# Local attention ahead of two feed-forward parts: attention recut into stacked 64-query blocks

## The chip, the cores and the metric

The kernel runs on one core of one Trainium2 chip. The time is device microseconds of one execution, as the median of three runs. The core's engines, as the profile names them, are PE (TensorE's products), PEld (its weight loads), DVE (VectorE), ACT (ScalarE), POOL (GpSimd) and SP (SyncE, which issues the transfers). Each works through its own queue in order and waits for the others by semaphores.

## What is computed

```python
def _attn_ref(q, k, v):                      # 2 batches, 8 heads, 576 tokens, 64 columns
    scores = 1.0 / np.sqrt(D) * np.matmul(q, k.transpose(0, 1, 3, 2))
    rel = pos[:, None] - pos[None, :]
    mask_plain = (rel >= 0) & (rel < 32)
    mask_dil = (rel >= 0) & (rel < 128) & (rel % 4 == 0)
    # heads 0 to 3 plain, heads 4 to 7 dilated; softmax of the masked scores; times v

def _moe_ref(x, domain_probs, w1, w2):       # 1152 tokens, 512 columns, 4 experts of 1024
    p = domain_probs / (domain_probs.sum(-1, keepdims=True) + 1e-09)
    for e in range(E):
        out += p[:, e:e + 1] * (np.maximum(x @ w1[e], 0.0) @ w2[e])

def _moe2_ref(x, w_in, w_out):               # 512 to 2048 and back
    h = x @ w_in
    return (h - np.tanh(h)) @ w_out
```

A query sees its own and the 31 keys before it, in a dilated head among the tokens of its own residue modulo 4.

## The kernel before

**Feed-forward.** The two parts together are twelve slices of 512 hidden columns (eight of the experts, four of the second part). The 1152 tokens are three groups of 384 (`T`). A slice's group is four `h_step`s (line 444: hidden block f, 12 products of 384 columns; operands are split into a high and a low part, three products for each of four blocks of input columns `kk`) and four `y_step`s (line 482: hidden block f against the second matrix, into three chunks of 128 tokens, 9 products of 512 columns). A hidden block leaves PSUM through ScalarE and VectorE (lines 451 and 452; in the second part a tanh and its difference, lines 458 to 471). `w_split` (lines 420 and 421) makes the high part of 1024 weight columns on ScalarE and the low part on GpSimd. `order` lists the (slice, group) steps: (0,0), (1,0), (0,1), (1,1) and so on, then slice by slice. `beside` says what is emitted behind each step: loads, splits, `x2_step` (line 520: transposes between the two parts), and attention.

**Attention.** It is cut into four units of rows of four tokens: 96 and 48 rows of the first batch, 48 and 96 of the second. A unit has four plain and four dilated heads. A head's queries are blocks of up to 96, each against a window of block + 32 keys. A `Pair` holds two heads, and each head goes through its stages by slots: `scores` (line 202 or 215, one product per block), the maximum on VectorE, `exps` (line 252, one exponential per block on ScalarE, that also sums), `sums` and the reciprocal (lines 262 and 271), `norm` on GpSimd (line 273), `p_transposes` (line 283) and `values` (line 300), and the result `xT` in high and low part (lines 317 and 318). In the first unit the mask joins the sum on TensorE as a product of an identity with the mask (line 198), in the others VectorE adds it on eviction (line 226). The first unit stands before all feed-forward steps; the other three are spread beside the first of them.

PSUM's eight banks are two `h`, three `y` and three `a`. Eleven products of zeros (line 598) come first.

Of the kernel before, what the change touches and what calls it, by code (L numbers as in the profile page):

```python
# [8 lines left out]
F32 = mybir.dt.float32  # L9
# [19 lines left out]
S = 576  # tokens of a batch  # L29
UNITS = [(0, 0, 96), (0, 96, 48), (1, 0, 48), (1, 48, 96)]  # batch, first row, rows of DIL tokens  # L30


def blocks(W, plain):
    """Blocks of a head of a unit, their queries and their keys."""
    M = BQ if plain else W
    return W * DIL // M, M, M + HALO


def _halves():
    """Each unit's plain heads, then its dilated ones, with their columns in the packed q, k, v."""  # L40
    out, at = [], [0, 0, 0]
    for unit in UNITS:
        for plain in (True, False):
# [12 lines left out]
def tile_local_attention_moe_tanhshrink(  # L56
    ctx: ExitStack,
    tc: tile.TileContext,
    q: bass.AP,  # the parts of a half unit side by side, see _pack
# [22 lines left out]
    xp = ctx.enter_context(tc.tile_pool(name="xp", bufs=NG * KD))  # L82
# [4 lines left out]
    ld = ctx.enter_context(tc.tile_pool(name="ld", bufs=2))  # L87
    sp = ctx.enter_context(tc.tile_pool(name="sp", bufs=3))
    st = ctx.enter_context(tc.tile_pool(name="st", bufs=4))
    ps_h = ctx.enter_context(tc.tile_pool(name="ps_h", bufs=2, space=bass.MemoryType.PSUM))  # L90
    ps_y = ctx.enter_context(tc.tile_pool(name="ps_y", bufs=3, space=bass.MemoryType.PSUM))
    ps_a = ctx.enter_context(tc.tile_pool(name="ps_a", bufs=3, space=bass.MemoryType.PSUM))

    PS = {"h": ps_h, "y": ps_y, "a": ps_a}
# [5 lines left out]
    ident = const.tile([128, 128], F32, name="ident")  # L100
    m_reg = const.tile([BQ, 128], F32, name="m_reg")
    m_first = const.tile([BQ, 128], F32, name="m_first")
    ident_b = const.tile([128, 128], BF16, name="ident_b")
# [72 lines left out]
    class Pair:  # L176
# [11 lines left out]
        def scores(self, a):  # L188
# [34 lines left out]
            if h.plain and first:  # L223
                cuts = [(0, 1, m_first), (1, nb, m_reg)]
# [455 lines left out]
```

## Time and profile before

| | us |
|---|---|
| median of three runs | 700.59 |
| lowest and highest | 698.97, 702.90 |
| span of the profiled execution | 697.1 |
| PE busy in it | 690.6 |
| DVE busy | 328.6 |
| ACT busy | 230.4 |
| POOL busy | 148.6 |

The runs' times and the span are of different executions; the median stands 3.5 us over the span, which begins with the first instruction and ends with the last. The busy time of PE counts the whole of an issued product, also where a neighbour overlaps it.

### The profile page before, as it was taken

The page shows a single profiled execution, that of the slowest core. Times are in us where ns is not written, and L with a number is a line of the kernel's source. Part 1 is how long each engine was busy: PE and PEld are TensorE (multiplying, and loading weights), DVE is VectorE, ACT ScalarE, POOL GpSimd, SP SyncE. Part 2 cuts the span into 40 slices and gives each one's busy share as a digit, 9 for nine tenths or more (in the row PEclk, how much of TensorE's full clock was granted, in tenths as well). Part 3 has the DMA queues.
Part 4 walks back from the last instruction along what each step waited for, and adds up shares of the span by engine and source line. Part 5 has one row for each costly group of instructions (what it writes and reads, how often), then busy time and mean ns, then how long its engine had stood idle before and what let it go on. Part 6 is the DMA issues. An engine that isn't in the chain of part 4 may idle for free.

```text
span 697.1 us, 9305 instructions
## 1 busy us (share of the span) xinstructions
PE 690.6 (99%) x3663; PEld 608.6 (87%) x3663; DVE 328.6 (47%) x599; ACT 230.4 (33%) x572; POOL 148.6 (21%) x106
## 2 busy tenths in 40 slices
PE   9999999999999999999999999999999999999997
PEld 5677788889999999999999999999999999999996
DVE  2258456322122222222222222488788699799433
ACT  3347574421412112122122121143454443344221
POOL 1236441200422112113122032022122122122000
PEclk8589999999999999999999999999999999999999
DMA  7024523000121102101101112032222133220111
GB/s 251 25 65 131 158 84 122 1 0 1 61 90 61 31 30 62 31 31 60 31 31 60 31 50 71 2 100 82 60 92 91 61 101 106 67 92 31 41 51 46
DMA packets 26908, 45.19 MB, mean 65 GB/s; under 512 B 2768, under 2 KB 14032, under 8 KB 26864
## 3 DMA queue, kind: packets, MB, share of 16 engines
q1 hardware_dynamic: 26864, 44.59, 20.3%
q8 instruction: 29, 0.48, 0.3%
q14 instruction: 15, 0.12, 0.1%
HBM read 42.22 MB, written 2.36 MB: 64 GB/s over the span
## 4 chain that ended last, share of the span: by engine, by line
PE 97%; DVE 2%; ACT 0%; issue 0%; DVEq 0%
PE bank_y L482 43%; PE bank_h L444 24%; PE bank_a L444 19%; PE bank_a L300 2%; PE bank_a L215 2%; PE bank_a L202 2%; PE bank_y L300 1%; PE bank_h L202 1%; PE bank_a L283 1%; PE bank_y L283 1%; PE bank_a L198 1%; PE bank_y L598 1%; PE bank_a L520 1%; DVE se L262 0%; PE bank_h L198 0%; DVE s L226 0%
## 5 line engine op out<-in xcount | busy, mean ns | idle before, releaser
L482 PE MATMUL bank_y<-whi,h 128*128 128x512 f32 x864 | 277.3, 393 | 0.0
L482 PEld LDWEIGHTS bank_y<-whi,h 128*128 128x128 f32 x864 | 162.2, 188 | 33.9
L482 PE MATMUL bank_y<-wlo,h 128*128 128x512 f32 x432 | 168.8, 391 | 0.0
L444 PE MATMUL bank_h<-x,whi 128*128 128x384 f32 x640 | 164.1, 337 | 0.0
L444 PE MATMUL bank_a<-x,whi 128*128 128x384 f32 x512 | 130.3, 335 | 0.0
L421 POOL TENSOR_TENSOR wlo<-raw,whi 128x1024 fp32r<-128x1024 f32 x32 | 76.4, 2389 | 238.6 <-ACT whi L420 238.6
L444 PEld LDWEIGHTS bank_h<-x,whi 128*128 128x128 f32 x640 | 115.3, 188 | 2.6
L444 PE MATMUL bank_h<-x,wlo 128*128 128x384 f32 x320 | 107.3, 335 | 0.0
L482 PEld LDWEIGHTS bank_y<-wlo,h 128*128 128x128 f32 x432 | 81.1, 188 | 15.7
L444 PEld LDWEIGHTS bank_a<-x,whi 128*128 128x128 f32 x512 | 92.7, 188 | 1.2
L498 DVE SCALAR_TENSOR_TENSOR acc<-bank_y,pn,acc 128x512 f32<-128x512 f32 x63 | 44.1, 749 | 93.4 <-PE bank_y L482 93.4
L444 PE MATMUL bank_a<-x,wlo 128*128 128x384 f32 x256 | 85.7, 335 | 0.0
L421 POOL TENSOR_TENSOR wlo<-t,whi 128x512 fp32r<-128x512 f32 x32 | 43.5, 1360 | 170.0 <-ACT whi L420 170.0
L452 DVE SCALAR_TENSOR_TENSOR h<-bank_h,h 128x384 fp32r<-128x384 f32 x60 | 33.4, 556 | 97.1 <-ACT h L451 97.1
L451 ACT ACTIVATE h<-bank_h 128x384 fp32r<-128x384 f32 x60 | 29.5, 491 | 146.6 <-PE bank_h L444 144.8
L444 PEld LDWEIGHTS bank_h<-x,wlo 128*128 128x128 f32 x320 | 60.1, 188 | 0.0
L451 ACT ACTIVATE h<-bank_a 128x384 fp32r<-128x384 f32 x36 | 17.7, 492 | 111.8 <-PE bank_a L444 111.8
L444 PEld LDWEIGHTS bank_a<-x,wlo 128*128 128x128 f32 x256 | 48.0, 188 | 0.0
L452 DVE SCALAR_TENSOR_TENSOR h<-bank_a,h 128x384 fp32r<-128x384 f32 x36 | 20.1, 557 | 53.6 <-ACT h L451 53.6
L420 ACT ACTIVATE whi<-t 128x512 fp32r<-128x512 f32 x32 | 20.3, 633 | 73.1 <-DVE t L404 73.1
L398 DVE SCALAR_TENSOR_TENSOR t<-raw,t 128x512 int32<-128x512 int32 x32 | 36.7, 1147 | 1.1
L420 ACT ACTIVATE whi<-raw 128x1024 fp32r<-128x1024 f32 x32 | 33.6, 1052 | 1.4 <-DMA raw<-in_moe_w_dram 1.4
(173 smaller groups left out, 572.6 us busy)
## 6 DMA issues: line engine op xcount, KB each, us to landing
raw<-in_moe_w_dram SPq DMA_DIRECT2D x32, 512.0 KB, 3.8
raw<-in_moe_w_in_dram SPq DMA_DIRECT2D x16, 512.0 KB, 3.6
raw<-in_moe_w_out_dram SPq DMA_DIRECT2D x16, 512.0 KB, 3.3
v<-in_v_dram SPq DMA_DIRECT2D x4, 512.0 KB, 4.2
out_dram<-oacc SPq DMA_DIRECT2D x8, 256.0 KB, 2.1
q<-in_q_dram SPq DMA_DIRECT2D x6, 192.0 KB, 2.6
q<-in_q_dram SPq DMA_DIRECT2D x3, 384.0 KB, 3.3
k<-in_k_dram SPq DMA_DIRECT2D x2, 512.0 KB, 5.3
```

The lines of the kernel that those rows point to most:

```text
L202: nc.tensor.matmul(out=sb[:M, j, :K], lhsT=h.q[r0:r0 + D, self.c, j * M:(j + 1) * M], rhs=h.k[r0:r0 + D, self.c, j * h.step:j * h.step + K ...
L215: nc.tensor.matmul(out=sb[:M, j, :K], lhsT=h.q[r0:r0 + D, self.c, j * M:(j + 1) * M], rhs=h.k[r0:r0 + D, self.c, j * h.step:j * h.step + K ...
L283: nc.tensor.transpose(pb[:K, j * M:(j + 1) * M], self.p[a][:M, j, :K], ident[:M, :M])
L300: nc.tensor.matmul(out=self.xb[D * a:D * a + D, j * M:(j + 1) * M], lhsT=h.v[:K, j, f0:f0 + D], rhs=self.pt[a][:K, j * M:(j + 1) * M], sta ...
L398: nc.vector.scalar_tensor_tensor(out=t, in0=low, scalar=29, in1=t, op0=ALU.logical_shift_right, op1=ALU.bitwise_or)
L420: nc.scalar.activation(out=hi, in_=raw, func=ACTF.Copy)
L421: nc.gpsimd.tensor_tensor(out=lo, in0=raw, in1=hi.bitcast(F32), op=ALU.subtract)
L444: nc.tensor.matmul(out=hb, lhsT=a, rhs=x[:, b_, :], start=(n == 0), stop=(n == 3 * KD - 1))
L451: nc.scalar.activation(out=ht[:, 0, :], in_=hb, func=ACTF.Relu)
L452: nc.vector.scalar_tensor_tensor(out=ht[:, 1, :], in0=hb, scalar=0.0, in1=ht[:, 0, :].bitcast(F32), op0=ALU.max, op1=ALU.subtract,)
L482: nc.tensor.matmul(out=state["y"][c], lhsT=a, rhs=b_, start=(f == 0 and n == 0), stop=(f == NF - 1 and n == 2),)
L498: nc.vector.scalar_tensor_tensor(out=acc[ch], in0=y, scalar=p, in1=acc[ch], op0=ALU.mult, op1=ALU.add)
```

## The change

Attention is cut by batch: plain heads as nine blocks of 64 queries, dilated heads as residues of 64, 64 and 16 rows. Blocks are stacked in pairs on the 128 partitions, so that a head is one tile of 128 x 5 x 96 scores (the tenth place of a plain head repeats its last block). `scores` takes two heads at once and alternates between them, one on the upper and one on the lower 64 rows, each into a bank of its own. The mask is added by VectorE for every unit; the maximum is subtracted by GpSimd; one exponential per head follows, and the sum is taken by VectorE. The transposed products leave through ScalarE alone. All of batch 0 stands before the feed-forward steps, with three of four input blocks of the first two hidden blocks put between its stages (`early_h`); batch 1 stands slot by slot beside the steps of (0,0) and (1,0). `y_step` goes chunk by chunk, all four hidden blocks at once. The banks are two each of `s`, `h`, `y` and `a`. Some weight splits of slice 0 go to VectorE, and the splits of slice 1 stand beside the first four steps.

```diff
-BQ = 96
+BQ = 64
+BK = BQ + HALO
+NST = 5
-UNITS = [(0, 0, 96), (0, 96, 48), (1, 0, 48), (1, 48, 96)]
+ROWS = S // DIL
+CUTS = [(0, BQ), (BQ, BQ), (2 * BQ, ROWS - 2 * BQ)]
...
+        def scores(self):
+            which = self.banks["s"]
+            self.sb = [
+                bank(which)[:, :NST * BK].rearrange("p (j c) -> p j c", c=BK) for _ in range(2)
+            ]
+            for part, j, qs, ks in self.h.scores(self.c):
+                M = qs.shape[1]
+                for a in range(2):
+                    nc.tensor.matmul(
+                        out=self.sb[a][part:part + M, j, :],
+                        lhsT=qs[D * a:D * a + D, :], rhs=ks[D * a:D * a + D, :],
+                        start=True, stop=True,
                     )
+        def largest(self, a):
...
+            nc.vector.scalar_tensor_tensor(
+                out=s, in0=self.sb[a], scalar=SCALE, in1=masks[self.h.plain],
+                op0=ALU.mult, op1=ALU.add,
+            )
+            nm = st.tile([128, NST], F32, tag="nm", name="nm")
+            nc.vector.tensor_reduce(out=nm, in_=s, axis=AX.X, op=ALU.max, negate=True)
+            nc.gpsimd.tensor_tensor(
+                out=s, in0=s, in1=nm.unsqueeze(2).to_broadcast([128, NST, BK]), op=ALU.add
+            )
...
+            nc.scalar.activation(out=p, in_=self.s[a], func=ACTF.Exp)
...
+            nc.vector.tensor_reduce(out=sm, in_=p, axis=AX.X, op=ALU.add)
+            nc.vector.tensor_scalar(out=sm, in0=sm, scalar1=1e-9, scalar2=None, op0=ALU.add)
...
+        def stages(self):
+            yield 7, 0, self.scores
+            for a in range(2):
+                for order, lag, emit in (
+                    (0, 1, self.largest), (1, 2, self.norm), (3, 3, self.p_transposes),
+                    (4, 1, self.exps),
+                ):
+                    yield order, a + lag, lambda emit=emit, a=a: emit(a)
+            yield 2, 5, self.values
...
-    def y_step(s, g, f, state):
...
+    def y_step(s, g, c, state):
+        y = bank("y")
+        for f in range(NF):
+            whi, wlo = wb(s, f)
...
+    EARLY = 2
+    def h_bank(s, g, f):
+        if (s, g) == (0, 0):
+            return "y" if f < EARLY else "h"
+        if s < 2 and g == 0:
+            return "h"
+        return "ha"[(s * NG * NF + g * NF + f) // 2 % 2]
...
+    def early_h(kk):
+        state = states[0, 0]
+        for f in range(EARLY):
+            h_products(0, 0, f, state, [kk])
+            state["done", f] = kk + 1
+    for kk in range(KD - 1):
+        slots[0][2 * kk + 6].append((5, lambda kk=kk: early_h(kk)))
...
+    for t, sc, engine in (
+        (3, early[0], nc.vector), (6, early[1], nc.gpsimd), (9, early[2], nc.vector),
+        (11, early[3], nc.gpsimd),
+    ):
+        slots[0][t].append((6, lambda sc=sc, engine=engine: w_split(*sc, engine=engine)))
+    for i, sc in enumerate(early[4:]):
+        put(i, lambda sc=sc: w_load(*sc))
+        put(i + 1, lambda sc=sc: w_split(*sc))
+    for t, emits in enumerate(slots[1]):
+        for _, emit in sorted(emits, key=lambda e: e[0]):
+            put(t, emit)
```

How the instructions stand on GpSimd around the first feed-forward steps (pn is a scaled tile of probabilities, wlo a low part of weights). Before:

```order
L421 TENSOR_TENSOR wlo_438<-raw_150,whi_437 128x1024
L273 TENSOR_TENSOR pn__503<-p_481,rs_501 96x256
L421 TENSOR_TENSOR wlo_512<-raw_152,whi_511 128x1024
L273 TENSOR_TENSOR pn__542<-p_505,rs_540 96x256
L273 TENSOR_TENSOR pn__565<-p_544,rs_563 96x256
L421 TENSOR_TENSOR wlo_577<-raw_154,whi_576 128x1024
```

One split stands between the scaled tiles there. Now, from the last split of slice 0 on (s is a tile of scores, nm its negated maximum):

```order
L459 TENSOR_TENSOR wlo_630<-raw_452,whi_629 128x1024
L228 MEMSET dq_668 128x32
L229 MEMSET dk_669 128x48
L459 TENSOR_TENSOR wlo_685<-raw_644,whi_684 128x1024
L304 TENSOR_TENSOR s_690<-s_690,nm_692 128x480
L459 TENSOR_TENSOR wlo_714<-raw_688,whi_713 128x1024
L304 TENSOR_TENSOR s_719<-s_719,nm_721 128x480
L326 TENSOR_TENSOR pn__729<-p_695,rs_727 128x480
```

Three splits and two subtractions stand ahead of the first scaled tile of batch 1 (729).

On TensorE the first hidden blocks and the attention beside them, before, from the first unit's last transposes on (L283 transposes, L300 values, L215 scores, L444 hidden blocks):

```order
L283 MATMUL bank_y<-ident,pn__423 128x96 x4
L300 MATMUL bank_y<-pt,v 64x96 x4
L215 MATMUL bank_a<-k,q 96x128 x2
L300 MATMUL bank_y<-pt,v 64x96 x4
L215 MATMUL bank_a<-k,q 96x128 x2
L444 MATMUL bank_h<-x,whi 128x384 x2
L444 MATMUL bank_h<-x,wlo 128x384
```

Scores of one head at a time stood between, and transposes of an earlier head behind each. Now, from the last products of the fourth hidden block of step (0,0) on (L483 hidden blocks, L335 transposes, L525 output chunks):

```order
L483 MATMUL bank_h<-x,whi 128x384 x2
L483 MATMUL bank_h<-x,wlo 128x384
L335 MATMUL bank_a<-ident,pn__729 96x128 x4
L525 MATMUL bank_y<-whi,h 128x512
L525 MATMUL bank_y<-wlo,h 128x512
L525 MATMUL bank_y<-whi,h 128x512 x2
```

The transposes of tile 729 stand between the hidden blocks and the first output chunk of step (0,0).

The start on TensorE, now, behind the products of zeros:

```order
L288 MATMUL bank_s<-pk,pq 64x96 x20
L288 MATMUL bank_h<-pk,pq 64x96 x20
L335 MATMUL bank_a<-ident,pn__220 96x128 x4
L335 MATMUL bank_a<-ident,pn__266 96x128 x4
L343 MATMUL bank_a<-ident,pn__220 96x128
L343 MATMUL bank_a<-ident,pn__266 96x128
L288 MATMUL bank_s<-dk,dq 64x96 x16
L288 MATMUL bank_s<-dk,dq 32x96 x8
L357 MATMUL bank_a<-pt,pv 64x64 x16
```

The third pair's scores stand behind the first pair's transposes; before, scores of six heads stood ahead of the first transposes.

## Rows read from the trace of the kernel before

**Rows 1.** the page: its first line and the chain by engine

```profile
span 697.1 us, 9305 instructions
...
PE 97%; DVE 2%; ACT 0%; issue 0%; DVEq 0%
```

**Rows 2.** windows: length, then each engine's busy us, clock, DMA share, GB/s

```profile
8.00:10.70 2.70, 2.70 (x15) 1.71 (x15) 1.01 (x3) 1.65 (x9) 0.00 (x0) 1.00 1.00 380
10.70:20.00 9.30, 9.30 (x31) 5.41 (x32) 1.95 (x8) 4.33 (x24) 2.07 (x2) 0.50 0.59 196
36.40:41.00 4.60, 4.60 (x25) 3.71 (x24) 3.01 (x8) 1.49 (x8) 2.07 (x2) 0.50 0.38 114
41.40:48.50 7.10, 6.44 (x56) 5.06 (x54) 4.62 (x11) 3.47 (x8) 3.36 (x2) 1.00 0.14 39
48.50:159.40 110.90, 109.97 (x726) 91.85 (x726) 57.57 (x146) 57.50 (x210) 35.21 (x31) 1.00 0.27 81
159.40:692.00 532.60, 532.60 (x2721) 485.81 (x2720) 252.12 (x400) 155.32 (x288) 100.96 (x56) 1.00 0.18 56
```

**Rows 3.** the chain in order of time: start us, us, what

```profile
48.59 2.33 PE bank_h L444 x12
...
159.42 8.34 PE bank_h L444 x48
167.77 8.20 PE bank_y L482 x36
...
691.85 1.78 DVE oacc L508 x3
```

**Rows 4.** TensorE in order of time: first product, and blocks of one head

```profile
4.87 0.26 PE L198 MATMUL bank_a<-m_first_b,ident_b 96*96 96x128 bf16 x1
...
43.92 0.67 PE L215 MATMUL bank_a<-k,q 64*96 64x128 f32 x4
44.52 0.55 PE L283 MATMUL bank_y<-ident,pn__423 96*128 96x96 f32 x4
...
118.98 1.11 PE L215 MATMUL bank_a<-k,q 64*96 64x128 f32 x8
120.02 0.55 PE L283 MATMUL bank_a<-ident,pn__1297 96*128 96x96 f32 x4
120.50 0.87 PE L300 MATMUL bank_a<-pt,v 128*64 128x96 f32 x8
121.30 0.44 PE L444 MATMUL bank_h<-x,whi 128*128 128x384 f32 x1
```

**Rows 5.** groups of instructions by form: busy us, mean ns, idle before

```profile
L421 POOL TENSOR_TENSOR wlo<-raw,whi 128x1024 fp32r<-128x1024 f32 x32 | 76.4, 2389 | 238.6 <-ACT whi L420 238.6
L420 ACT ACTIVATE whi<-raw 128x1024 fp32r<-128x1024 f32 x32 | 33.6, 1052 | 1.4 <-DMA raw<-in_moe_w_dram 1.4
L226 DVE SCALAR_TENSOR_TENSOR s<-bank_a,m_reg 96x512 f32<-96x512 f32 x8 | 5.5, 687 | 5.9 <-PE bank_a L215 5.8
```

**Rows 6.** in order of time: VectorE's small step alone and beside GpSimd

```profile
37.18 0.15 DVE L262 TENSOR_SCALAR se<-sm 96x4 f32<-96x4 f32 x1
37.79 1.04 POOL L273 TENSOR_TENSOR pn__367<-p,rs 96x512 f32<-96x512 f32 x1 [5.02 <-DVE rs L271]
37.98 0.87 DVE L262 TENSOR_SCALAR se<-sm 96x4 f32<-96x4 f32 x1
```

**Rows 7.** in order of time: second part, a group's last hidden block

```profile
585.53 0.39 PE L482 MATMUL bank_y<-whi,h 128*128 128x512 f32 x1
...
586.90 0.53 ACT L470 ACTIVATE h<-gt 128x384 fp32r<-128x384 f32 x1 [0.21 <-DVE gt L462]
...
587.46 0.56 DVE L471 TENSOR_TENSOR h<-gt,h 128x384 fp32r<-128x384 f32 x1
```

**Rows 8.** groups by form: a hidden block's eviction

```profile
L451 ACT ACTIVATE h<-bank_h 128x384 fp32r<-128x384 f32 x60 | 29.5, 491 | 146.6 <-PE bank_h L444 144.8 <-PE bank_a L283 1.9
L452 DVE SCALAR_TENSOR_TENSOR h<-bank_h,h 128x384 fp32r<-128x384 f32 x60 | 33.4, 556 | 97.1 <-ACT h L451 97.1
```

More of the change, by code (lines that the diff above doesn't have):

```diff
@@ L41, in _halves @@
     out, at = [], [0, 0, 0]
-    for unit in UNITS:
-        for plain in (True, False):
+    for b in range(2):
+        for unit, plain in [((b, 0, ROWS), True)] + [((b, *cut), False) for cut in CUTS]:
             out.append((unit, plain, tuple(at)))
@@ L317, in values @@
[L317 to L318 removed]
+            pb = bank(self.banks["t"])
+            for i in range(2):
+                nc.tensor.transpose(pb[:BK, i * 128:(i + 1) * 128], self.p[i][:, n, :], ident)
+            last = sp.tile([128, 256], F32, tag="pl", name="last", bufs=2)
+            nc.scalar.activation(out=last[:BK], in_=pb[:BK, :256], func=ACTF.Copy)
+            self.last = last
@@ new lines, in values @@
+        def values(self):
+            h = self.h
+            xb = [bank(self.banks["x"]) for _ in range(2)]
+            for blk, t, i, o, n in h.values():
+                for a in range(2):
+                    f0 = (2 * self.c + a) * D
+                    pt = self.pt[a][:BK, t:t + n] if t < 512 else (
+                        self.last[:BK, t - 512 + a * 128:t - 512 + a * 128 + n]
+                    )
+                    nc.tensor.matmul(
+                        out=xb[i][D * a:D * a + D, o:o + n],
+                        lhsT=h.v[:, blk, f0:f0 + D], rhs=pt, start=True, stop=True,
+                    )
+            x = xT[self.kk]
+            for i in range(2):
+                (hi, n, r), (lo, _, _) = (h.spans(x[:, j])[i] for j in range(2))
+                src = xb[i][:, :n]
+                if r is not None:
+                    src = src.rearrange("c (r p) -> c r p", r=r)
+                nc.scalar.activation(out=hi, in_=src, func=ACTF.Copy)
+                nc.vector.tensor_tensor(out=lo, in0=src, in1=hi.bitcast(F32), op=ALU.subtract)
@@ new lines, in tile_local_attention_moe_tanhshrink @@
+    kinds = [kind(b) for b in range(2) for kind in (Plain, Dilated)]
+    slots = [[[] for _ in range(SLOTS)] for _ in range(2)]
+    for b in range(2):
+        for n in range(4):
+            banks = {"s": "sh"[n % 2], "t": "a", "x": "a"} if b == 0 else {"s": "s", "t": "a", "x": "a"}
+            for order_, slot, emit in Pair(kinds[2 * b + n // 2], n % 2, banks).stages():
+                slots[b][2 * n + slot].append((order_, emit))
+    def early_h(kk):
[3 more added lines that the diff above has]
+            state["done", f] = kk + 1
@@ L592, in tile_local_attention_moe_tanhshrink @@
         nc.vector.memset(zero, 0.0)
-        for half in halves[:2]:
-            half.load_qk()
-            half.load_v()
+        kinds[0].load_qk(0)
+        kinds[0].load_qk(1)
+        w_load(*early[0])
+        kinds[0].load_v()
+        w_load(*early[1])
         idle = bank("y")
```

495 lines of the change are left out of this document (220 added, 275 removed).

## Prediction

> **What bounds the kernel now.** I read the page's first lines and its chain first, then the stretches, then the chain in order of time. The chain lies on TensorE for 97% of a span of 697.1 us [rows 1], so the question is how long TensorE works or waits in each stage, and nothing else. The stages [rows 2, 3]: until 48.6 us no feed-forward product runs, TensorE does the first unit's attention (a third of all: 96 of 288 rows); from 48.6 to 159.4 the other two thirds stand between feed-forward steps; from 159.4 to 691.9 feed-forward work alone; then 5.2 us of last sums and stores.
>
> The reader should see three more things in these rows. A slice's group costs 8.34 + 8.20 = 16.54 us and they follow without a gap [rows 3]; 36 of them make 595.4. The stretch of 532.4 us [rows 2] holds 32 (529.3), so the transposes between the two feed-forward parts cost 3.1. Four groups (66.2) lie between 48.6 and 159.4, so attention takes 44.7 us there. And the granted clock is 1.00 up to 10.7 us and 0.50 (1.2 GHz of 2.4) from then on, while TensorE's rows leave no idle time; it is back after the stretch from 36.4 to 41, 4.6 us of transposes and value products without masks between them [rows 2]. So the span is 48.6 + 595.4 + 3.1 + 44.7 + 5.2 = 697.0. The median of the runs lies 3.5 us above the profiled span; I add that at the end.
>
> **What an attention product costs at full clock.** Every product with float32 operands is two passes. Four score passes of 128 columns take 0.60 up to the next block, eight take 1.04 [rows 4]: 0.11 a pass, 0.0825 for 96 columns, and 0.16 for the change of block. Four transposes of 96 columns take 0.48 with such a change, 0.08 each, so 0.11 for 128; eight value passes of 96 columns 0.80, so 0.055 for 64. By these passes the products of the two thirds come to 31.4; the other 13.3 of the 44.7 are the edges of 72 blocks (24 heads, three blocks each), 0.19 an edge.
>
> **Batch 1's attention, beside steps (0,0) and (1,0).** The change removes the mask products, widens 128-column windows to pairs of 96 (88 score products a batch: 2 x 20 plain, 2 x 24 dilated) and does two heads a block. Score passes: 88 x 2 x 0.0825 = 14.5. Transposes 40 x 0.11 = 4.4. Value passes: 136 of 64 columns at 0.055 and 32 of 16 at no more than 0.05, 9.1. Sixteen edges 3.0. That is 31.0. Nothing in the rows shows two heads' passes alternating between row halves. The upper end is the row's own 0.0825 a pass; the lower end is 0.055, the shortest pass seen, of the same 64 weight columns. I take 0.0825, the nearer shape.
>
> New waits come on top. GpSimd now subtracts the maximum as well as scaling, and it is in order. Its rows as the change orders them begin with the last split of slice 0, the split of (1,0), the first head's subtraction, the split of (1,1), the second subtraction, then the first scaling. Splits cost 2.39, ScalarE's copy ahead of each 1.05 [rows 5], a GpSimd step of 480 columns 1.0 (1.04 for 512 [rows 6]), an exponential of 480 columns 0.6 (a little over half of that copy of 1024). Counted from the first feed-forward product that completes the early ones, the second hidden block's eviction lets the copy for (1,0) start near 4.0; split to 7.5, subtraction to 8.5, exponential, an eviction (0.5) and the next copy to 10.9, split to 13.3, subtraction and scaling to 15.3. TensorE reaches the first transposes of batch 1 after 0.5 + 3.3 + 0.5 + 2.1 + 3.3 + 2.1 (the rests of two hidden blocks, scores, two whole blocks of 12 x 0.174) and edges, 12.4: a wait of 2.9. The next head's scaling stands behind one more split, near 21.0, while TensorE has only one output chunk (2.7) to do: a wait of 2.4. Three times transposes follow values at once and need the same two banks back, an eviction by ScalarE and VectorE, 1.1 each: 3.3. Batch 1 thus takes 31.0 + 5.3 + 3.3 = 39.6, for half the attention, against 44.7 for two thirds. Whatever TensorE has behind these waits, the output products of step (0,0) among them, is queued, as it is in order.
>
> **The start, with all of batch 0.** Now the stages of eight heads come before the first full feed-forward step, and they are a chain through four engines. VectorE per head: scale and mask 0.65 (0.687 for 512 columns [rows 5]), the maximum the same, later the sum the same and two small steps 0.4; I call these 1.35 and 1.05. The first score product needs half as much again of queries and keys; it starts at 4.87 now [rows 4], I take 5.5. Pair 1's scores end at 8.8, pair 2's at 12.1. VectorE works through heads 1 to 3 until 15.5, then holds for a weight split whose ScalarE copy stands behind a transposed copy and an exponential: 18.7. Heads 4 and 5, after pair 3's scores (to 21.4), their sums and the first values' evictions: 25.3. Heads 3 and 4's transposes wait for those evictions; with them, six early feed-forward products (1.0) and pair 4's scores TensorE is at 31.2. From there VectorE 1.35 + 1.05 + 1.0 + 1.35, head 8's subtraction, exponential, sum and scaling 3.9, pair 3's values to be evicted 1.3, transposes 0.9, ScalarE's two copies round a weight copy 2.65, values 2.6, evictions 2.0: 18.1, so 49.3. A VectorE step of 4 columns took 0.87 beside a GpSimd step and 0.15 else [rows 6]; the change puts such steps beside GpSimd for every head, I add 0.7: 50.
>
> TensorE stands idle from 12.1 to about 17.5 in this chain but for 0.4 of transposes. The clock fell at 10.7 after a stretch that had no gap at all [rows 2], so I let it fall here, and come back, as in the rows, after some 4.6 us of unbroken products: pair 3's scores and pair 1's values (5.9 at full clock) then cost 4 more. The start ends at 54. The 18 feed-forward products that it already does (18 at 8.34 / 48 = 0.174, 3.1) are taken off the later work, and cancel the 3.1 of transposes. Lower end 46 (shorter passes, no fall of the clock). Upper end: all of it at half clock, when TensorE itself binds: 2 x (14.5 + 4.4 + 9.1 + 3.1) + 5.5 + 2 = 69.
>
> **The feed-forward steps in their new order.** An output chunk now takes all four hidden blocks at once. The last block's two halves are ready 1.90 and 2.49 us after the first output product starts [rows 7]; before, products of three chunks covered them, now nine products of 8.20 / 36 = 0.228 (2.05). Weight loads that can no longer run ahead cost about 0.25, in the 12 groups of the second part: 3. At the three groups with transposes the fourth hidden block needs a bank that is still being evicted (0.49 + 0.56 [rows 8]): 1.0 each, 3. Other groups keep their banks in time. Together 6, ends 0 and 12.
>
> **Sum.** 54 + 595.4 + 39.6 + 6 + 5.2 = 700.2, with the 3.5 about 704 us, half a per cent over the median. A measurement of this kernel can tell about that half per cent from no change. Less TensorE work (masks gone, fewer edges) is given back in longer waits at the start.
>
> **Rivals.** First, the two heads' score passes run side by side, so that a pass costs as little as 0.055. For it: they lie on different row halves and banks. Against it: no row has the pattern. The start loses 3, batch 1's scores 4.8, but the wait on GpSimd grows by 2.6, since that chain hardly moves: 699. The Trainium skill, TensorEngine Tiling (Array Packing), under Key Properties and Performance Considerations, states that tiles on different rows can load weights and multiply in parallel, up to twice as fast with 64 rows; no run here shows it yet. By that rule score work would halve rather than lose a third, and most of the rest would go into the same wait on GpSimd, an estimate of 698.
>
> Second, the same and a clock that stays at 1.00, because the early products and denser score blocks fill the gap at 12 to 17 us: the start ends 4 sooner, 695, faster. It decides if the granted clock from 12 to 25 us reads 1.00. For it speaks that the clock held through all later stretches; against it that it fell without any gap.
>
> Third, slower: the clock stays at 0.50 throughout the start and TensorE binds it, up to 69, the sum 719. It decides if pairs take 13 us each or more. Against it: dense stretches brought the clock back at 41 us.
>
> Fourth, the change does not bring its feed-forward products early, as the early blocks wait for a weight split: nothing beyond 3 us either way, inside the forecast's spread.
>
> **Chances.** The forecast 0.47, its own range 697 to 713 (0.20 within half a per cent, 0.27 over); side by side 0.15 (0.11 within, 0.04 faster); side by side at full clock 0.23 (faster); half clock 0.15 (slower). So faster 0.27, same 0.31, slower 0.42. The range from 689 to 718 takes in the second rival with some spread and reaches to the third.
>
> **What would show it.** Right: the first product of step (0,0) that completes a block starts near 54, with a half-clock stretch inside; TensorE waits for GpSimd at batch 1's first two transposes; small waits for hidden blocks in the second part; 16.5 a group in between. Wrong: score passes of two heads overlapping in time, a clock of 1.00 through the start, or an interleaved stretch without waits on GpSimd.

## The result and the profile after

The changed kernel takes **690.0 us** (median of four runs, 689.2 to 690.7) against 700.8 us before (four runs, 699.0 to 702.9): a ratio of 0.984, 95% interval 0.981 to 0.986. It is faster by 1.6%, where 704 was forecast and 0.42 lay on slower. The range from 689 to 718 holds the time at its lower edge.

The page's first line and its chain by engine, as in [rows 1]:

```profile
span 687.9 us, 9361 instructions
...
PE 85%; DVE 6%; DMA 3%; issue 2%; ACT 1%; POOL 1%; SPq 1%; DVEq 0%; POOLq 0%; ACTq 0%
```

TensorE still carries the chain, but 15% of it now lies on others; it was 3%. TensorE in order of time, as in [rows 4] (the bracket is the idle time ahead of a row and what ended it):

```profile
4.76 1.06 PE L288 MATMUL bank_s<-pk,pq 64*64 64x96 f32 x40
...
18.72 1.51 PE L288 MATMUL bank_s<-dk,dq 64*64 64x96 f32 x32 [1.24 <-DMA dk<-in_k_dram]
...
42.72 0.44 PE L483 MATMUL bank_y<-x,whi 128*128 128x384 f32 x1 [0.78 <-ACT x L367]
...
44.98 0.62 PE L483 MATMUL bank_y<-x,whi 128*128 128x384 f32 x2
...
52.85 1.87 PE L288 MATMUL bank_s<-pk,pq 64*64 64x96 f32 x38 [4.67 <-DVE s L298]
...
59.98 0.64 PE L335 MATMUL bank_a<-ident,pn__729 128*96 128x128 f32 x4 [1.31 <-POOL dq L228]
...
65.37 0.64 PE L335 MATMUL bank_a<-ident,pn__801 128*96 128x128 f32 x4 [1.99 <-POOL pn__801 L326]
...
76.50 1.22 PE L288 MATMUL bank_s<-dk,dq 64*64 64x96 f32 x48
...
79.94 1.15 PE L357 MATMUL bank_a<-pt,pv 96*64 96x64 f32 x32
80.92 0.29 PE L357 MATMUL bank_a<-last,pv 96*64 96x64 f32 x4
84.21 0.61 PE L335 MATMUL bank_a<-ident,pn__968 128*96 128x128 f32 x4 [3.00 <-DVE x L368]
...
94.67 0.61 PE L335 MATMUL bank_a<-ident,pn__1097 128*96 128x128 f32 x4 [1.91 <-DVE x L368]
```

Three things are to be seen. The 40 score passes of a plain pair, two passes for each of ten blocks of two heads, take 1.06 us: 0.026 a pass, where the forecast had 0.0825 and a lower end of 0.055. The first product of step (0,0) that completes a hidden block starts at 42.72, not at 54 (the row at 44.98 completes the second hidden block; it serves below as the mark at which the start is over). And the waits of batch 1 are there, at more places than forecast.

The granted clock by stretches, as in [rows 2], and the chain in order of time, as in [rows 3]:

```profile
10.60:27.50 16.90, 11.08 (x110) 8.66 (x110) 11.29 (x22) 7.11 (x14) 8.03 (x11) 0.50 1.00 259
27.70:51.40 23.70, 16.14 (x273) 12.99 (x272) 15.19 (x28) 12.11 (x22) 13.48 (x12) 1.00 0.68 148
51.60:58.20 6.60, 5.35 (x49) 5.13 (x50) 2.70 (x6) 1.10 (x2) 2.53 (x2) 0.50 1.04 302
85.70:88.90 3.20, 3.20 (x14) 3.03 (x13) 0.46 (x1) 0.87 (x3) 0.00 (x0) 0.50 0.00 0
96.00:99.20 3.20, 3.20 (x13) 3.04 (x13) 0.12 (x1) 0.49 (x1) 0.00 (x0) 0.50 0.02 5
```

```profile
7.30 11.29 DMA dk<-in_k_dram
...
109.53 4.18 PE bank_h L483 x24
...
117.88 8.20 PE bank_y L525 x36
...
591.36 8.61 PE bank_y L525 x36
...
675.65 8.39 PE bank_y L525 x36
```

The clock falls near 10.5 us, as it did before, but comes back at 27.6 instead of 41, and falls three more times in batch 1, behind the waits of 4.67, 3.00 and 1.91 above. In the start a transfer stands on the chain for 11 us. From 109.5 us on it is feed-forward work alone, at 16.54 us a group as before, and in the second part an output step takes 8.36 to 8.63 us instead of 8.20.

### The profile page after: what moved, and what is told of

The parts are those of the page before. It is cut to its first block, busy times and chain, and to the rows that moved or that the text cites. A ratio compares the mean times of both kernels' runs of the same rounds, so it can differ in the third digit from the quotient of the medians.

```text
span 687.9 us, 9361 instructions
## 1 busy us (share of the span) xinstructions
PE 652.1 (95%) x3839; PEld 580.4 (84%) x3839; DVE 323.4 (47%) x533; ACT 205.1 (30%) x376; POOL 149.6 (22%) x117
## 4 chain that ended last, share of the span: by engine, by line
PE 85%; DVE 6%; DMA 3%; issue 2%; ACT 1%; POOL 1%; SPq 1%; DVEq 0%; POOLq 0%; ACTq 0%
PE bank_y L525 40%; PE bank_h L483 21%; PE bank_a L483 21%; DMA dk<-in_k_dram 2%; DMA raw<-in_moe_w_dram 1%; PE bank_a L335 1%; DVE t L433 1%; SPq L235 1%; POOL s L304 1%; PE bank_s L288 1%; DVE t L436 1%; DVE acc L537 1%; DVE t L429 1%; PE bank_y L670 1%; ACT h L494 1%
## 5 line engine op out<-in xcount | busy, mean ns | idle before, releaser
L525 PE MATMUL bank_y<-whi,h 128*128 128x512 f32 x864 | 277.5, 394 | 0.0
L525 PEld LDWEIGHTS bank_y<-whi,h 128*128 128x128 f32 x864 | 160.6, 188 | 39.1 <-DVE h L507 3.1
L525 PE MATMUL bank_y<-wlo,h 128*128 128x512 f32 x432 | 169.0, 391 | 0.0
L483 PE MATMUL bank_h<-x,whi 128*128 128x384 f32 x592 | 154.2, 341 | 0.0
L483 PE MATMUL bank_a<-x,whi 128*128 128x384 f32 x544 | 138.7, 335 | 2.6 <-DVE h L495 1.7
L459 POOL TENSOR_TENSOR wlo<-raw,whi 128x1024 fp32r<-128x1024 f32 x30 | 71.7, 2393 | 279.2 <-ACT whi L458 279.2
L483 PEld LDWEIGHTS bank_h<-x,whi 128*128 128x128 f32 x592 | 109.8, 192 | 3.0 <-issue 0.2
L483 PE MATMUL bank_h<-x,wlo 128*128 128x384 f32 x296 | 101.0, 341 | 0.0
L483 PEld LDWEIGHTS bank_a<-x,whi 128*128 128x128 f32 x544 | 98.0, 188 | 3.3 <-DVE h L495 2.2
L525 PEld LDWEIGHTS bank_y<-wlo,h 128*128 128x128 f32 x432 | 81.1, 188 | 15.4
L483 PE MATMUL bank_a<-x,wlo 128*128 128x384 f32 x272 | 90.9, 334 | 0.0
L494 ACT ACTIVATE h<-bank_h 128x384 fp32r<-128x384 f32 x50 | 24.5, 490 | 206.5 <-PE bank_h L483 206.5
L495 DVE SCALAR_TENSOR_TENSOR h<-bank_h,h 128x384 fp32r<-128x384 f32 x50 | 27.8, 557 | 106.6 <-ACT h L494 106.6
L495 DVE SCALAR_TENSOR_TENSOR h<-bank_a,h 128x384 fp32r<-128x384 f32 x44 | 24.5, 558 | 69.0 <-ACT h L494 69.0
L483 PEld LDWEIGHTS bank_h<-x,wlo 128*128 128x128 f32 x296 | 56.8, 192 | 0.0
L483 PEld LDWEIGHTS bank_a<-x,wlo 128*128 128x128 f32 x272 | 51.1, 188 | 0.0
## 6 DMA issues: line engine op xcount, KB each, us to landing
pv<-in_v_dram SPq DMA_DIRECT2D x2, 864.0 KB, 11.3
```

The lines of the kernel that those rows point to most:

```text
L459: (engine or nc.gpsimd).tensor_tensor(out=lo, in0=raw, in1=hi.bitcast(F32), op=ALU.subtract)
L483: nc.tensor.matmul(out=state["bank", f], lhsT=a, rhs=x[:, b_, :], start=(kk == 0 and n == 0), stop=(kk == KD - 1 and n == 2),)
L494: nc.scalar.activation(out=ht[:, 0, :], in_=hb, func=ACTF.Relu)
L495: nc.vector.scalar_tensor_tensor(out=ht[:, 1, :], in0=hb, scalar=0.0, in1=ht[:, 0, :].bitcast(F32), op0=ALU.max, op1=ALU.subtract,)
L525: nc.tensor.matmul(out=y, lhsT=a, rhs=b_, start=(f == 0 and n == 0), stop=(f == NF - 1 and n == 2),)
```

## The experiments

All start from the changed kernel. Times are medians of four or more runs, and differences of 1 to 2 us can lie within their spread (the runs of one kernel lie 1 to 6 us apart); each ratio is to the kernel before, run on the same chip.

| run | us | ratio, 95% interval | mean granted clock, profiled run |
|---|---|---|---|
| changed kernel | 690.0 | 0.984 (0.981, 0.986) | 0.977 |
| heads apart | 696.8 | 0.992 (0.990, 0.995) | 0.969 |
| parts apart | 697.3 | 0.995 (0.993, 0.997) | 0.973 |
| both apart | 714.9 | 1.017 (1.012, 1.022) | 0.953 |
| scores and values apart | 715.7 | 1.020 (1.017, 1.024) | 0.964 |
| weights first | 689.6 | 0.985 (0.981, 0.988) | 0.972 |
| splits behind | 687.0 | 0.982 (0.978, 0.986) | 0.980 |
| tail of groups | 685.8 | 0.979 (0.975, 0.982) | 0.975 |
| filled start | 688.4 | 0.984 (0.980, 0.987) | 0.988 |
| three together | 682.4 | 0.974 (0.969, 0.978) | 0.987 |
| dilated first | 684.3 | 0.976 (0.972, 0.980) | 0.980 |
| filled batch 1 | 677.4 | 0.966 (0.962, 0.971) | 1.000 |
| both apart, filled | 692.1 | 0.987 (0.981, 0.992) | 0.995 |

### Why a score pass is so short: heads apart, parts apart, both apart

```diff
-            for part, j, qs, ks in self.h.scores(self.c):
-                for a in range(2):
+            for a in range(2):
+                for part, j, qs, ks in self.h.scores(self.c):
```

That is heads apart. Parts apart keeps the alternating heads and sorts the blocks, and both apart has the two edits:

```diff
-            for part, j, qs, ks in self.h.scores(self.c):
+            for part, j, qs, ks in sorted(self.h.scores(self.c), key=lambda e: e[0]):
```

> All score products of a pair's first head stand before those of the second, so neighbours differ only in the half of the output partitions they write, no longer in the half of the rows they read. In the changed kernel the 40 passes of a plain pair take 1.06 us, 0.026 each, where the forecast had 0.0825 and a lower end of 0.055. Theory: four quarters of the array work at the same time, two by rows and two by columns; then 40 passes take about 2.1 us here, batch 1's 176 passes 4.4 us more than now, part of it hidden in waits, and the time is 692 to 698. Rival A, a narrow pass is short by itself whatever stands beside it: 1.06 us and 690. Rival B, only rows count: 2.1 us here as well, but 1.06 in the run that keeps the heads alternating.

> Heads alternate as before, but all blocks that write the lower output partitions stand before those that write the upper ones, so neighbours differ in rows alone. Theory of four quarters: 40 passes of a plain pair take about 2.1 us, time 692 to 698. Rival A (a narrow pass is short by itself): 1.06 us, 690. Rival B (only rows count): 1.06 us, 690, while the run with the heads apart is slower. A fourth possibility, only columns count: 2.1 or more here and 1.06 with the heads apart.

> Heads apart and partitions apart: neighbours share rows and columns of the array. Theory of four quarters: one pass at a time, 3.3 us for the 40 passes by the forecast's 0.0825, up to 4.2 if a pass alone is four times 0.026; batch 1's 176 passes then cost 10 to 14 us more than now, the start up to as much, about half of it hidden in waits: 698 to 708. Rival A (a narrow pass is short by itself): 1.06 us and 690. If a time near the forecast's 704 comes out, the forecast failed by the price of a score pass and by little else.

The last dilated pair's 48 passes at a granted clock of 1.00, in the runs with heads apart, parts apart and both apart; the same block of the changed kernel is the 1.22 at 76.50 above:

```profile
80.92 2.28 PE L288 MATMUL bank_s<-dk,dq 64*64 64x96 f32 x48
```

```profile
82.76 2.28 PE L288 MATMUL bank_s<-dk,dq 64*64 64x96 f32 x48
```

```profile
95.88 4.42 PE L288 MATMUL bank_s<-dk,dq 64*64 64x96 f32 x48
```

1.22, 2.28, 2.28, 4.42: take away the alternation of heads or that of output halves, and the block takes 1.9 times as long; take away both, 3.6 times. So passes on four quarters of the array overlap. Rival A (short by itself) and rival B (rows only) are out. The 40 passes of a plain pair, for which 2.1 us were expected with one alternation and 3.3 to 4.2 with none, take 1.60 and 2.69 at full clock, against 1.06. One thing stays open: two heads lie on different row halves and in different banks, and no run puts both row halves into one bank. The Trainium skill, TensorEngine Tiling (Array Packing), under Available Configurations, lists four tiles of 64 x 64, and under Theoretical Speedup gives up to twice for a dimension of at most 64. The rows agree: 1.9 times by one dimension and 3.6 by two, 1.7 and 2.5 for plain pairs. The prediction had taken from that page the rows alone.

Both apart was expected at 698 to 708 and took 714.9. What was not counted is the clock. Windows of that run, two of its seven stretches at 0.50 and the sum of all (the longest, 20.3 us, lies in the start):

```profile
49.30:59.40 10.10, 10.10 (x56) 9.44 (x57) 4.64 (x7) 1.92 (x3) 4.11 (x4) 0.50 0.21 59
...
76.60:90.10 13.50, 13.50 (x63) 9.60 (x61) 2.82 (x6) 1.95 (x4) 6.21 (x5) 0.50 0.15 47
...
sum 63.50, PE 59.38 PEld 50.17 DVE 22.47 ACT 15.28 POOL 24.40; mean PE 8.48 PEld 7.17 DVE 3.21 ACT 2.18 POOL 3.49
```

The seven make 63.5 us at half clock; the four of the changed kernel make 29.9. So it was open how much of the 25 us is passes and how much clock; the last run bounds that.

### Value products

```diff
-            for blk, t, i, o, n in h.values():
-                for a in range(2):
+            for a in range(2):
+                for blk, t, i, o, n in h.values():
```

> As the run with both apart, and the value products of a pair's first head stand before the second's, so that neighbours no longer alternate between the two halves of the output partitions. In the changed kernel 36 value passes of a plain pair take 1.27 us, 0.035 each, where the forecast had 0.055. Theory: column halves overlap in these too, so 36 passes take 2.0 to 2.6 us, batch 1's values 4 to 6 us more than now, and the time is 3 to 8 us over the run with only the scores apart: 702 to 714. Rival A: 1.27 us, and the same time as that run.

The second plain pair of batch 1 in that run (18 + 13 of its 36 passes; the rest stands between them):

```profile
108.24 1.20 PE L357 MATMUL bank_a<-pt,pv 96*64 96x64 f32 x18
...
109.33 0.92 PE L357 MATMUL bank_a<-pt,pv 96*64 96x64 f32 x13
110.09 0.28 PE L357 MATMUL bank_a<-last,pv 96*64 96x64 f32 x2
```

The pair takes about 2.1 us (108.24 to 110.4) instead of 1.27 (79.94 to 81.21 above): 0.058 a pass instead of 0.035. The forecast's 0.055 was the price of a pass that alternates with nothing. The whole kernel lost only 0.8 us by it, less than the spread of the runs (714.5 to 717.3 against 710.0 to 715.9) and below the 3 to 8 expected: the profiled run spends less time at half clock than its neighbour (mean 0.964 against 0.953), and waits for VectorE's evictions ahead of transposes shrink, from 7.0 to 5.2 us in all. What of that is cause and what chance, these runs don't tell.

### The waits of batch 1: weights first, splits behind

```diff
     for i, sc in enumerate(early[4:]):
-        put(i, lambda sc=sc: w_load(*sc))
-        put(i + 1, lambda sc=sc: w_split(*sc))
+        put(i - 1, lambda sc=sc: w_load(*sc))
     for t, emits in enumerate(slots[1]):
         for _, emit in sorted(emits, key=lambda e: e[0]):
             put(t, emit)
+    for i, sc in enumerate(early[4:]):
+        put(i + 1, lambda sc=sc: w_split(*sc))
```

Weights first is the line of the load alone; splits behind is all of it.

> The loads of slice 1's second chunk and of those after it stand one step earlier on SyncE, ahead of batch 1's dilated queries and keys; nothing else moves. In the changed kernel that load is issued at 50.0 us, behind six loads that wait for the buffers of the pair scored at 44 us, lands at 56.6, and the split that needs it ends on GpSimd at 58.0, ahead of the first scaled tile of batch 1. Theory: the load is the releaser there; the split ends before 54, TensorE's wait of 1.31 us ahead of the first transposes goes and the next waits shrink: 2 to 4 us less, 686 to 688. Rival: GpSimd's order alone holds TensorE, its split, two subtractions and a scaling add up anyway, and the scores of the second pair still start near 52.8: 689 to 691.

> As the run with the weights first, and each split of slice 1 stands behind the subtraction, exponential and scaling of its step instead of ahead of them. Theory: in-order GpSimd is the second releaser: the wait of 4.67 us ahead of the second pair's scores, which goes back through an eviction and an exponential to the subtraction behind a split of 2.35, falls by 2 or more, the waits of 1.31 and 1.99 at the first two transposes go, and with shorter gaps the granted clock does not fall at 51.5 us, which costs some 2.6 us now: 683 to 686. Rival: the waits move to VectorE's chain (two maxima, two sums, evictions) and little is left to gain: 687 to 690.

Weights first, GpSimd and then TensorE in order of time:

```profile
53.30 2.35 POOL L459 TENSOR_TENSOR wlo<-raw,whi 128x1024 fp32r<-128x1024 f32 x1 [2.04 <-ACT whi L458]
```

```profile
53.48 1.87 PE L288 MATMUL bank_s<-pk,pq 64*64 64x96 f32 x38 [4.67 <-DVE s L298]
...
65.16 0.64 PE L335 MATMUL bank_a<-ident,pn__801 128*96 128x128 f32 x4 [2.69 <-POOL pn__801 L326]
```

The load is no longer late: the split ends at 55.7 instead of 58.0, though its start of batch 1 is 0.6 us later. The wait of 1.31 is gone, and the next one is 2.69 instead of 1.99: the time is the same. The rival held; the load stood on the chain, but only in parallel with GpSimd's order. The clock has a part in it: behind the 2.69 it fell here (about 65.5 to 69 us), which it did not behind the 1.99. Splits behind:

```profile
51.42 1.87 PE L288 MATMUL bank_s<-pk,pq 64*64 64x96 f32 x38 [4.35 <-DVE s L298]
...
62.28 0.64 PE L335 MATMUL bank_a<-ident,pn__797 128*96 128x128 f32 x4 [1.71 <-POOL pn__797 L326]
```

687.0, at the lower end of the rival's range, and of these 3.0 us the profiled run has 1.1 already at the end of the start (43.9 instead of 45.0), which the edit does not touch; from there to step (0,1) it takes 62.5 us instead of 64.55. The wait of 4.67 fell only to 4.35: the second head's maximum stands on VectorE behind the eviction of a hidden block, which stands on ScalarE behind the first head's exponential. GpSimd's part of the split went behind the subtraction, and the exponential starts 4.4 us after the second hidden block (48.28 - 43.89) instead of 5.7 (50.66 - 44.98), but ScalarE's copy for the same split went between the exponential and the eviction and takes most of that back. ScalarE in that run:

```profile
48.28 0.60 ACT L313 ACTIVATE p<-s 128x480 f32<-128x480 f32 x1 [3.08 <-POOL s L304]
48.80 1.04 ACT L458 ACTIVATE whi<-raw 128x1024 fp32r<-128x1024 f32 x1
49.74 0.47 ACT L494 ACTIVATE h<-bank_h 128x384 fp32r<-128x384 f32 x1
```

No run puts that copy behind the eviction. The clock fell here too, at 50.4 us.

### The second part's output steps

```diff
+        last = NF - 1
...
+        elif c == 0:
+            todo = [(i, f) for i in range(2) for f in range(last)] + [(0, last)]
+        elif c == 1:
+            todo = [(1, last)]
...
+        for i, f in todo:
+            if f == 0:
+                state["y", i] = bank("s" if i == 2 and slices[s][2] is None else "y")
...
-        tb = bank("a")[:, :T]
+        tb = bank("s")[:, :T]
```

> Only in the second part: the first two output chunks of a group take hidden blocks 0 to 2 before either takes the last one, the third chunk and the transposes between the parts write the two banks that scores no longer need. From 109.4 us to the last product 574.7 us pass now, 34 groups of 16.54 make 562.4 and the transposes 3.1: 9.2 us are waits (the forecast had 6). Theory: the 0.16 to 0.43 that a group's output part takes over 8.20 goes (about 3.5 in all), and the three waits of 0.84 to 0.92 behind the transposes (2.6) with it: 5 to 6 us less, 684 to 686. Rival: VectorE's weight decoding holds the evictions there, whatever the banks: 688 to 690.

One group's output step there, chain in order of time:

```profile
604.72 5.62 PE bank_y L535 x24
610.34 2.72 PE bank_s L535 x12
```

8.34 where the same step took 8.6. From the first product of step (0,1) to the last one 569.5 us pass instead of 574.5, and 685.8 us is in the theory's range: the new waits of that stretch cost at least these 5 us (4.2 in the medians).

### The clock of the start: filled start

```diff
+    def fill(n):
+        for _ in range(n):
+            nc.tensor.matmul(
+                out=idle[0].rearrange("p (a b) -> p a b", b=32), lhsT=zero,
+                rhs=zero[:, :32].unsqueeze(1).to_broadcast([128, 16, 32]), start=True, stop=True,
+            )
+    for t, order_, n in ((0, 7.5, 6), (2, 7.5, 10), (3, 3.5, 8), (4, 3.5, 5), (5, 2.5, 5)):
+        slots[0][t].append((order_, lambda n=n: fill(n)))
```

> Products of zeros with all 128 weight columns take the place of those with 32 at the start, and 34 more stand in the gaps of batch 0's first two pairs (at 6, 8.5, 11.7, 15 and 22 us). The granted clock is 0.50 from 10.5 to 27.6 us in the changed kernel. Theory: it falls because TensorE does too little there; with the gaps filled it stays at 1.00 or comes back sooner, the transposes and early products of 23.5 to 27.8 us take half, and the start ends 2 to 4 us earlier: 686 to 688. Rival A: it falls near 10.5 us in any case, as it did before the change without a gap: 690. Rival B: the clock stays up and the chain of loads, VectorE and GpSimd binds all the same: 689 to 690 at a clock of 1.00.

The first eleven products of zeros also go from 32 to 128 weight columns here, so the run does not part that from the filled gaps. The start's window in that run, and where its second hidden block is completed (44.98 in the changed kernel):

```profile
0.00:40.90 40.90, 32.07 (x450) 20.58 (x450) 28.39 (x61) 19.65 (x34) 21.69 (x37) 1.00 0.87 236
```

```profile
41.93 0.62 PE L483 MATMUL bank_y<-x,whi 128*128 128x384 f32 x2
```

The clock stays at 1.00 and the start ends 3.05 us earlier, so it need not fall near 10.5 us: rival A is out. The size is less sure than that. With the start untouched, the same product stands at 43.89 (splits behind), 45.04 (tail of groups) and 45.62 (weights first); with the start filled, at 42.39 (filled batch 1) and 45.48 (three together, below). So where the filling worked it gave some 2.7 us (44.9 on the mean against 42.2), and in one execution of three it did not work. At the end 1.6 us are left (688.4, just over the expected 686 to 688), and the runs overlap (688.0 to 690.5 against 689.2 to 690.7): batch 1 has four stretches at half clock there instead of three.

### Together: three together, dilated first, filled batch 1

> The splits behind, the tail of groups and the filled start together. Alone, their spans were 3.3, 4.3 and 2.0 us shorter than the changed kernel's 687.9, at three different places of the program. If these costs lie one behind the other on TensorE, they add: a span near 678.3, a median of 680 to 682. Rival: the start that ends earlier meets the same loads and splits of slice 1, so that the start's gain is lost in batch 1 again, as in the filled start alone (3.1 us earlier at the end of the start, 2.0 at the end): 682 to 684.

682.4: the rival's range. The three gains don't add fully; 7.1 us of span remain of 9.6. The rival's way is not what the profiled execution shows, though. The start's gain is missing at the end of the start already: the second hidden block is completed at 45.48, the third pair's scores had waited for their transfer until 19.30 (17.15 in the filled start), and the clock fell in spite of the zeros:

```profile
32.30:35.70 3.40, 3.40 (x16) 2.90 (x18) 2.09 (x7) 1.79 (x4) 1.98 (x2) 0.50 0.98 238
```

```profile
45.48 0.62 PE L483 MATMUL bank_y<-x,whi 128*128 128x384 f32 x2
```

From there to step (0,1) pass 62.0 us, as with the splits behind alone (62.5), so batch 1 took nothing of it back.

Dilated first:

```diff
         put_load(b, 0, lambda d=dilated: d.load_qk(0))
+            put_load(0, 0, plain.load_v)
+            put_load(0, 0, lambda: w_load(0, 0))
...
+            put_load(0, 2, lambda: w_load(0, 1))
+            put_load(0, 2, dilated.load_v)
...
-        w_load(*early[0])
-        kinds[0].load_v()
-        w_load(*early[1])
```

> As the three together, and in the start the loads of the first dilated queries and keys stand ahead of the values and of the first two weight chunks (the first split moves back by one step). In the changed kernel these loads are asked for from 5.9 us on, with 1.9 MB ahead of them on the queues, and end at 18.6; the first dilated scores wait for them twice. Theory: the transfers' rate binds that stretch (DMA engines busy above 0.95 of 4.8 to 23.5 us), the order is what can be changed: the first dilated scores are done near 12 to 14 instead of 20.2, VectorE's chain moves up, the start ends 3 to 5 us earlier than with the three together, and so does the end. Rival: VectorE binds (some 20 us of steps for eight heads), the early weights come late in their place: within 1.5 us of the three together.

TensorE and then VectorE in that run:

```profile
15.72 1.22 PE L288 MATMUL bank_s<-dk,dq 64*64 64x96 f32 x48
```

```profile
18.43 1.23 DVE L459 TENSOR_TENSOR wlo<-raw,whi 128x1024 fp32r<-128x1024 f32 x1 [3.15 <-ACT whi L458]
19.58 0.65 DVE L298 SCALAR_TENSOR_TENSOR s<-bank_s,mask_False 128x480 f32<-128x480 f32 x1
```

No gain: 684.3 (681.7 to 685.9), near the rival. The dilated scores are done at 16.9, but the first weight chunk now lands late, its split stands on VectorE ahead of their maximum, and VectorE waits 3.15 us for it. The transfers only changed places. The clock was at 0.50 from about 24 to 27.5 and 31 to 37.5 us in this start, so a part of the loss may be the clock's.

Filled batch 1:

```diff
+    for t, order_, n in ((2, 6.5, 18), (7, 2.9, 12), (9, 2.9, 8)):
+        slots[1][t].append((order_, lambda n=n: fill(n, "y")))
```

That is added to the three together; these products write a bank of `y` that is free there.

> As the three together, and products of zeros also stand in three waits of batch 1 (18 ahead of the second pair's scores, 12 and 8 ahead of the transposes that follow values). In the run with the splits behind, the granted clock fell to 0.50 for 6.8, 3.4 and 3.4 us behind just these waits (50.4, 81.1 and 91.4 us). Theory: it falls because of the waits; with products in them it stays at 1.00, and half of these 13.6 us, less what was waited in them anyway, comes back: 3 to 6 us less than with the three together. Rival A: it falls because of the narrow attention products themselves, fill or not: no gain, or a loss of 1 to 2 by products in the way. Rival B: the clock stays up, but the chain behind the waits (GpSimd, VectorE) binds again: less than 2.

Its windows of the start and of batch 1, and the place of the former wait of 4.67:

```profile
0.00:41.00 41.00, 32.20 (x449) 20.55 (x450) 28.05 (x60) 19.65 (x34) 21.32 (x36) 1.00 0.89 245
41.00:102.00 61.00, 57.42 (x588) 45.67 (x589) 34.18 (x63) 24.07 (x44) 27.73 (x25) 1.00 0.29 92
```

```profile
49.93 1.05 PE L288 MATMUL bank_s<-pk,pq 64*64 64x96 f32 x38 [0.46 <-DVE s L298]
```

677.4, 5.0 below the three together: the theory held. From the end of the start to step (0,1) pass 56.9 us (42.39 to 99.25) instead of 62.0. The clock is 1.00 in the profiled run and 0.993 to 0.997 on the mean of the other three, with the same attention products: at these places it fell because of the waits. That narrow products alone never lower it is not shown; the next run has such a place. This is the fastest version, 3.4% below the kernel before (0.962 to 0.971).

### Passes and clock parted: both apart, filled

> The version with the filled start, the filled batch 1, the splits behind and the tail of groups (677.4 us, clock 1.00 throughout), with the score products of both heads and both output halves apart again. In the changed kernel that edit alone cost 25 us, with 64 us at half clock instead of 30. It parts what the passes themselves cost from what the clock costs. Passes at full clock: 80 plain ones of a batch at 0.061 instead of 0.026 and 96 dilated ones at 0.092 instead of 0.025, 9 us in batch 1 and 9 in the start, of which a third or so takes the place of zero products and waits. Theory: with the waits filled the clock stays near 1.00, and the time is 12 to 18 us over 677.4: 689 to 695. Rival A: the narrow products alone on the array lower the clock whatever stands between: 698 to 704 and a granted clock that falls as often as in the run with both apart. Rival B: the passes are hidden in the waits and the 25 us were the clock's: under 686.

692.1, 14.7 over the same kernel with the heads and parts alternating: the theory's range. One stretch at 0.50 is left (47.9 to 54.5 us). It begins inside a block of score passes in a row, ahead of which TensorE had waited 0.80 and 0.28 us and no more, so there rival A has a point:

```profile
46.38 3.74 PE L288 MATMUL bank_s<-pk,pq 64*64 64x96 f32 x40
```

Groups of score products by form in the run with batch 1 filled (alternating) and in this one (busy us, then mean ns of one):

```profile
L288 PE MATMUL bank_s<-pk,pq 64*64 64x96 f32 x120 | 3.5, 248 | 0.5 <-DVE s L298 0.5
L288 PE MATMUL bank_s<-dk,dq 64*64 64x96 f32 x96 | 2.9, 250 | 0.7 <-DMA dk<-in_k_dram 0.4 <-DVE s L298 0.3
```

```profile
L288 PE MATMUL bank_s<-dk,dq 64*64 64x96 f32 x96 | 10.4, 249 | 0.0
L288 PE MATMUL bank_s<-pk,pq 64*64 64x96 f32 x120 | 9.6, 272 | 0.0
```

One dilated pass lasts the same 250 ns in both (some of the plain ones ran at half clock, hence 272); what differs is how many are under way at once, so the same 96 occupy 2.9 or 10.4 us. Of the 25 us that both apart cost in the changed kernel, about 15 are thus passes in a row, at most 3.3 of them the half clock of the stretch that is left (6.6 us), and about 10 remain, by subtraction, for the clock and the waits behind it.

## Why the prediction was wrong, step by step

**What bounds the kernel.** Right in kind: TensorE, stage by stage. The stages, forecast and measured:

| | forecast | measured |
|---|---|---|
| start, until step (0,0) completes its first block | 54 | 42.7 |
| batch 1 beside steps (0,0) and (1,0), net of their products | 39.6 | 36.8 |
| transposes and new waits from 109.5 us on | 3.1 + 6 | 12.1 |
| last sums and stores | 5.2 | 3.8 |
| median over the span | 3.5 | 2.1 |

Batch 1 is 109.53 - 42.72 less two steps of 16.54 without their early 3.1; 12.1 is 574.5 less 34 groups of 16.54. The differences, -11.3, -2.8, +3.0, -1.4 and -1.4, make the 14 us that the forecast lay over.

**The step that failed: "I take 0.0825, the nearer shape", and its lower end of 0.055.** Passes in a row do cost that: by the blocks of both apart, filled (2.69 us for 40 plain passes and 4.42 for 48 dilated ones), 0.081 on a batch's average. But the change does not issue them in a row. Each neighbour lies on another quarter, and the 176 passes of a batch cost 0.026 each at full clock. In the forecast's own sum this one size takes 10 us off batch 1, and in the start up to 7.6 off pairs 1, 3 and 4 on its chain (3.3 + 3.9 + 3.9 against 1.06 + 1.22 + 1.22): 686, or 689 if the wait on GpSimd grows by the 2.6 of the first rival, instead of 704. The lower end had a place only for passes that shorten each other by a third. Values were mis-sized in the same way: 9.1 us a batch forecast, 5.6 measured (two blocks of 1.27 and two of 1.51).

**The first rival** had the mechanism, but half of it: rows, not columns. Its wait on GpSimd was to grow from 5.3 to 7.9 at the first two transposes. The waits up to there make 7.97 (4.67 + 1.31 + 1.99), but only 3.30 of them end with GpSimd; the 4.67 ends with VectorE, which waits by way of ScalarE for the first subtraction on GpSimd. **The second rival** gave the side and nearly the time (695) for a reason that did not occur: the clock did read 0.50 from 10.6 to 27.5. The run with the start filled shows what it would have been worth, some 2.7 us at the start's end where the forecast took 4.

**Waits and clock in batch 1** were too small, and hid part of the gain. Forecast: products 31.0, waits 8.6, half clock none. Measured: waits of 4.67, 1.31, 1.99, 0.99, 3.00 and 1.91, 13.9; half clock, half of TensorE's 5.35, 3.20 and 3.20 us in the three windows, 5.9; with 0.3 at the first block, 16.7 are left for the products, 14.3 less than forecast: 10 of scores, 3.5 of values, and little of the 3.0 of edges. The two waits that were forecast at the first transposes (2.9 and 2.4) are there, 1.31 and 1.99 long. The largest one, ahead of the second pair's scores, was not foreseen: the pair needs both score banks, and one is held by a maximum behind an eviction, an exponential and a subtraction, which stands behind a split on GpSimd. The forecast has that row of steps (to 10.9 after its mark), but lets it hold only the transposes.

**The start** was forecast as a chain of VectorE, GpSimd and ScalarE. That the third pair's scores would wait for a transfer until 18.6 us was left out: the DMA engines' share stands at 1.00 there, and in the run with the dilated loads first another order only moved the wait to the weights. (The upper end of the start adds up to 69.7, not 69; nothing hangs on it.)

**The new feed-forward order** was right in its two terms, which measure 5.9 against 6: three waits of 0.84 to 0.91 behind the transposes against three of 1.0, and 0.16 to 0.43 a group in the second part against 0.25. The other 3 us lie in the stretch of the transposes (423.92 to 498.82), which the forecast had at 3.1 + 3; no run says what they are. The run on the tail of groups took 5 us out again. The early products came early, so the fourth rival is out; half clock through the whole start, the third, did not come.

## What to carry to other kernels

Products that use a quarter of TensorE's array are priced by what stands beside them: alternate rows and output halves from one product to the next. Here, with a bank of its own for each row half, four passes cost 0.10 to 0.11 us together, where one in a row cost 0.067 (plain) to 0.092 (dilated). When such a change makes TensorE's work shorter, look at once for what it then waits for, since each gap can also cost the clock of what comes behind it; here products of zeros in three gaps gave back more (5 us) than moving the splits that made one of them (2 to 3 us). A price read from a row holds only for the neighbours that the row had.

## What the runs showed of the hardware that was not expected

- Products of at most 64 x 64 on different quarters overlapped with float32 operands: 48 dilated passes of 96 columns (a third of them 64 x 32) in 1.22 us, 2.28 with one alternation, 4.42 with none.
- Plain blocks, all 64 x 64, gained less than dilated ones: 2.69 us for 40 passes in a row against 1.06, 2.5 times, and 1.60 with one alternation. Why is open.
- Products of zeros kept the granted clock at 1.00 through the start (40.9 us) in two of three executions, with 3.4 us at 0.50 in the third, and through all of batch 1 in one. Without them it fell behind three of the six waits of batch 1 (4.67, 3.00 and 1.91) and not behind the others (1.31, 1.99 and 0.99). In the runs tail of groups and filled start it fell behind a wait of 2.01 as well, so the length of a wait alone does not tell.
- VectorE's normalising product of 128 x 36 probabilities took 2.06 us at 43.97, while a GpSimd split ran from 43.60 to 45.97, much as its step of 4 columns in [rows 6]. It took 2.01 to 2.06 in every run, each time beside a split, so no row shows it alone.
